# Of every two indirect transfers of GpSimd, only the first waits for a TensorE step

## The chip, the cores and the metric

The kernel runs on one core of one Trainium2 chip. The metric is the device time of one execution in microseconds (us), a median of several runs. A profiled execution has a span, from its first to its last instruction, and a time of its own that is a little longer. The engines are named as the profile names them: PE (TensorE; PEld its weight loads), DVE (VectorE), ACT (ScalarE), POOL (GpSimd) and SP (SyncE, which only issues DMAs here).

## What is computed

The first half is a gated recurrence over time, the second a mixture of eight experts in which each row goes to one expert.

```python
# x, f_logit: (4, 5056, 256); lower_bound: (256)
f = lower_bound + (1 - lower_bound) * sigmoid(f_logit)
for t in range(S):                       # S = 5056
    h = f[:, t] * h + (1 - f[:, t]) * x[:, t]
    y[:, t] = h
# y as N = 20224 rows of D = 256; E = 8 experts, F = 1024
xn, en = y / (norm(y) + 1e-6), emb / (norm(emb) + 1e-6)
logits = xn @ en.T / tau
e = argmax(logits); gate = softmax(logits)[e]
out[row] = gate * (relu(y[row] @ w1[e]) @ w2[e])
```

## The kernel before

**Chunks.** The 20224 rows are taken in 40 chunks of up to 512. For a chunk, SP loads f_logit and x (three buffers of each), TensorE transposes both so that features lie on partitions (L782, L816), ScalarE makes the gate (tanh, L793, and a scaled identity, L799), VectorE forms the product (L824) and scans along time (L840). ScalarE squares the result (L852). The result is turned back into rows, early on by TensorE, later by copies in bf16 (L861) and a DMA transpose on SP (L871), into the buffers `Yt`.

**Groups.** One or two chunks are a group. `route_` finds each row's expert and the slot that the row gets in its expert's region of a scratch in DRAM, `Xs`; `gate_` makes the gate weight, and then issues the scatters: for each block of 128 rows one indirect DMA on GpSimd's queue (L1109), which sends rows with gate and row number (544 bytes) to their slots. A full group has eight scatters, j = 0 to 7; there are 158 in all. `update_` writes, at chosen groups, a table of which expert's region the next tiles lie in.

**Tiles.** A tile is 256 rows of one expert. 81 tiles are always run (`NM`), a few more only if a counter asks for them. For tile n, SP loads the rows transposed from `Xs` (L1331; six buffers `ys`) and gate and row number (L1341, `xm`). TensorE multiplies by the expert's first matrix (L1434) in two steps, ScalarE and VectorE take the relu (L1455, L1460), TensorE multiplies by the second matrix (L1482) in four steps, ScalarE scales the first 128 rows by the gate (L1497) and VectorE the second 128 (L1501), into one of six buffers `osb`. Two indirect DMAs on GpSimd's queue (L1507), s = 0 and s = 1, send these to their rows of the output; there are 162.

**The order.** Nothing is ordered by hand. Each instruction group is an `Op` with dependencies, and `schedule` simulates all five engines with costs that are written beside the operations (an indirect transfer 1280 ns, a transfer's landing `DMA_FIX` 1900 ns) and places the operations one after another by readiness and priority. Each engine then runs its list in the order so found, and `resolve` turns each dependency into a semaphore wait, leaving out those that are implied by earlier waits. When an operation of GpSimd that carries a DMA and has `paced` set is placed at the simulated time s, it gets one more dependency, after its place is fixed: on the last TensorE step whose simulated end is not later than s (`PACE` is 0). On the chip GpSimd therefore does not run ahead of TensorE further than in the simulation. Before the change all scatters are paced, and all outputs except those of the last four tiles. GpSimd's other work is a set of constants at the start and the load of the sixteen expert matrices (L762).

Of the kernel before, what the change touches and what calls it, by code (L numbers as in the profile page):

```python
# [34 lines left out]
class Prog:  # L35
# [93 lines left out]
    def schedule(self, first, caps):  # L129
# [43 lines left out]
        while True:  # L173
            best = None
            for e in free:
                while wait[e] and wait[e][0][0] <= free[e]:
                    t, p, i, o = heapq.heappop(wait[e])
                    heapq.heappush(avail[e], (p, i, o))
                if avail[e]:
                    s = free[e]  # L180
                elif wait[e]:
                    s = wait[e][0][0]
# [6 lines left out]
            s, e = best  # L189
# [6 lines left out]
            if soon is not None:  # L196
                wait[e].remove(soon)
                heapq.heapify(wait[e])
                s, p, i, o = soon
            elif avail[e]:  # L200
                p, i, o = heapq.heappop(avail[e])
            else:
                t, p, i, o = heapq.heappop(wait[e])
            gap = s - free[e]
            if e == "pe" and s < self.COLD and gap > self.IDLE:
                room = [(t, q) for q, t in enumerate(frees) if t is not None and t <= s - self.IDLE]
                if room and ready_at(self.warm_on) is not None:
                    t, q = min(room)
                    a = max(t, free[e], ready_at(self.warm_on))
                    n = int((s - a - self.REST) / (self.UNIT * (2 if s < self.COLD else 1)))  # L210
# [29 lines left out]
            if o.dma is not None:  # L240
                bus = max(bus, free[e]) + o.nbytes / self.DMA_RATE
                o.end = max(bus, free[e]) + self.DMA_FIX
                if e == "pool" and o.paced:
                    o.end = min(o.end, free[e] + self.DMA_FIX)
            else:
                o.end = free[e] + self.LAG[e]
# [126 lines left out]
def bass_hgrn_recurrence__then__cosine_router_kernel(  # L373
# [41 lines left out]
    with ExitStack() as es:  # L415
# [491 lines left out]
        def views(g, hr=None):  # L907
            cc = groups[g]
            K, nb = len(cc), nof(cc[0]) // P
            J = K * nb  # L910
            q = g % R2
            o = bof[g][1] * 8

            def rt_():
                return bank[hr.b][:, 0:392].rearrange("p (b c) -> p b c", b=4)[:, 0:nb, :]

            def Lv():
                return rt_()[:, :, 0:64].rearrange("p b (k e) -> p b k e", k=2)[:, :, 0:K, 0:8]

            def Nv():  # L920
                return rt_()[:, :, 64:98:32][:, :, 0:K]

            def v4(t, o=0):
                return t[:, o * 8 : (o + J) * 8].rearrange("p (b k e) -> p b k e", b=nb, k=K)

            def v3(t, o=0):
                return t[:, o : o + J].rearrange("p (b k) -> p b k", b=nb)

            def bc(t, o=0):
                return v3(t, o).unsqueeze(3).to_broadcast([P, nb, K, 8])  # L930

            return K, nb, J, q, Lv, Nv, v4, v3, bc
# [115 lines left out]
        def gate_(bi):  # L1048
# [32 lines left out]
            for g in gg:  # L1081
                K, nb, J = views(g)[0:3]
                v3 = views(g)[7]
                o = bof[g][1] * 8
# [16 lines left out]
            for g in gg:  # L1101
                K, nb, J = views(g)[0:3]
                o = bof[g][1] * 8
                for b in range(nb):
                    for k_ in range(K):
                        j = b * K + k_
                        sc = op(
                            "pool",
                            lambda e, j=o + j, i=o + k_ * 4 + b: e.indirect_dma_start(  # L1109
                                out=Xs[:, :],  # L1110
                                out_offset=bass.IndirectOffsetOnAxis(
                                    ap=sli[y][:, j : j + 1], axis=0
                                ),
                                in_=Yt[y][:].bitcast(I32)[:, i, :],
                                in_offset=None,
                            ),
                            1280, r=[("Yt", y, k_, 0), ("Yt", y, k_, 1), ("Ytg", y), ("Yti", y), ("ytz", y), ("sli", y)],
                            w=[("Xs", g)], dma=f"sc{y}_{k_}", nbytes=100000, chain=False,
                        )
                        sc.paced = True  # L1120


        def update_(u, g, last):
# [188 lines left out]
        NM = N // T + E // 4  # L1312
# [5 lines left out]
        def tile_(j, u, g, n):  # L1318
# [105 lines left out]
            for mp in range(2):  # L1424
# [26 lines left out]
                for m, h in ((2 * mp, hh[0]), (2 * mp + 1, hh[1])):  # L1451
                    o = hT[qh][:, 2 * m : 2 * m + 2, :].rearrange("p f c -> p (f c)")
                    if m % 2 == 0:
                        act(
                            lambda e, o=o, h=h: e.activation(o, bank[h.b][:], AF.Relu), 512,  # L1455
                            h=h, w=[("hT", qh, m)], prio=EVP(pr.prio), tag="mid",
                        )
                    else:
                        dve(
                            lambda e, o=o, h=h: e.tensor_scalar(  # L1460
                                o, bank[h.b][:], 0.0, None, op0=ALU.max
                            ),
# [41 lines left out]
            for s in range(2):  # L1504
                sc = op(
                    "pool",
                    lambda e, s=s: e.indirect_dma_start(  # L1507
                        out=out[:, :],
                        out_offset=bass.IndirectOffsetOnAxis(
                            ap=xm[qx][:, s, 1:2], axis=0  # L1510
                        ),
                        in_=osb[qo][:, s, :],
                        in_offset=None,
                        bounds_check=N - 1,
                        oob_is_err=False,
                    ),
                    1280, r=[("osb", qo, s)] + xk, w=[("out", j, s)], dma=f"od{qo}_{s}",
                    nbytes=170000, prio=OUTP(pr.prio),
                )
                sc.paced = n < NM - 4  # L1520


        last_of = {cc[-1]: g for g, cc in enumerate(groups)}
# [20 lines left out]
        def put(j, n):  # L1544
            u, g = avail[j]
            pr.prio = 10000 + n
            tile_(j, u, g, n)

        for c in range(NCH):
            pr.prio = c  # L1550
            if c >= 2:
                load(c)
            F_(c)
            X_(c)
            Y_(c)
            if c == 0:
                for i in range(2 * E):
                    wload(i, c)
            if c == 1:
                late_constants()  # L1560
            if c in last_of:
                g = last_of[c]
                route_(g)
                bi, gi = bof[g]
                if g == batches[bi][-1]:
                    gate_(bi)
                for u, at in enumerate(ups):
                    if at == g:
                        update_(u, g, u == len(ups) - 1)
# [63 lines left out]
```

## Time and profile before

| | us |
|---|---|
| three timed runs | 559.63, 563.5, 564.1 |
| their median | 563.5 |
| the profiled execution's own time | 565.46 |
| its span | 563.7 |
| PE busy / PEld busy | 475.2 / 382.8 |
| DVE busy | 359.5 |
| ACT busy | 321.1 |
| POOL busy | 331.9 |

Busy time is summed over the span; engines work beside each other, so the rows don't add up to it. The granted TensorE clock was 0.963 of full speed on average. The last chunk's scan lies near 332 us, so that the last 230 us hold tiles alone, with the rest of the scatters between their outputs.

### The profile page before, as it was taken

To read this page: it belongs to the slowest core of one execution; us is meant where nothing else is said; L and a number is where in the kernel's file an instruction comes from. 1 tells how busy PE (TensorE), PEld (TensorE's weight loads), DVE (VectorE), ACT (ScalarE), POOL (GpSimd) and SP (SyncE) were. 2 spreads that over 40 slices of the span, in tenths; PEclk is the share of its full clock that TensorE was granted. 3 is DMA by queue.
4 is the path that set the end of the run, shared out by engine and by line. 5 is a ranking of instruction groups with operands and counts; after the bars stand their busy time and mean duration, and the time that the engine had idled before them with its cause. 6 is when DMAs were issued, how large, how long until landed. Compare 5 with 4: busy or idle time off the path is not lost. (4 is left out here: it accounts for less than half of the span.)

```text
span 563.7 us, 12407 instructions
## 1 busy us (share of the span) xinstructions
PE 475.2 (84%) x4106; PEld 382.8 (68%) x4106; DVE 359.5 (64%) x1075; ACT 321.1 (57%) x573; POOL 331.9 (59%) x388
## 2 busy tenths in 40 slices
PE   7796778979798789887887988888988897978994
PEld 4474557757577567656765657777777776867894
DVE  7869978877787667875877876533444343443452
ACT  4878768877787566757776753333333332333342
POOL 6164565655665565564666665656665666655555
PEclk8969988998998889999999999999999999999998
DMA  8999999999999788879896543353343433444422
GB/s 243 302 311 313 318 254 311 287 254 219 206 234 241 202 205 190 238 172 219 221 241 133 117 92 99 113 127 105 100 110 95 110 88 100 106 109 101 106 65 74
DMA packets 119681, 100.49 MB, mean 178 GB/s; under 512 B 96884, under 2 KB 98687, under 8 KB 119616
## 3 DMA queue, kind: packets, MB, share of 16 engines
q1 hardware_dynamic: 101664, 59.38, 42.5%
q0 software_dynamic: 16224, 40.26, 26.2%
q8 instruction: 36, 0.59, 0.5%
q10 hardware_dynamic: 1728, 0.01, 0.2%
q14 instruction: 29, 0.24, 0.2%
HBM read 59.21 MB, written 32.93 MB: 163 GB/s over the span
## 5 line engine op out<-in xcount | busy, mean ns | idle before, releaser
L1507 POOL DMA_INDIRECT out_dram<-osb,xm x162 | 160.7, 992 | 107.6 <-issue 34.0
L1109 POOL DMA_INDIRECT XsScratch<-Yt,sli x158 | 152.2, 963 | 105.6 <-issue 26.6
L1434 PE MATMUL bank<-ys,wall 128*128 128x256 bf16 (+1 forms) x1392 | 174.4, 271 | 19.1 <-issue 13.4
L1482 PE MATMUL bank<-wall,hT 128*128 x1296 | 172.8, 274 | 15.0 <-issue 12.6
L1460 DVE TENSOR_SCALAR hT<-bank 128x512 bf16<-128x512 f32 x162 | 108.4, 684 | 100.8 <-remote 46.0
L1434 PEld LDWEIGHTS bank<-ys,wall 128*128 x1392 | 147.5, 145 | 34.9 <-issue 24.7
L1455 ACT ACTIVATE hT<-bank 128x512 bf16<-128x512 f32 x162 | 94.0, 597 | 114.1 <-remote 49.5
L1482 PEld LDWEIGHTS bank<-wall,hT 128*128 128x128 bf16 x1296 | 124.4, 98 | 42.9 <-issue 23.0
L840 DVE TENSOR_TENSOR_SCAN hb<-fg,hb,bank 128x512 f32<-128x512 f32 (+4 forms) x78 | 95.9, 1236 | 0.1
L1501 DVE TENSOR_SCALAR osb<-bank,xm 128x256 f32<-128x256 f32 x81 | 38.8, 479 | 59.7 <-ACT osb L1497 32.6
L1497 ACT ACTIVATE osb<-bank,xm 128x256 f32<-128x256 f32 x81 | 38.4, 475 | 59.7 <-remote 17.4
L816 PE MATMUL bank<-ident,xin 128*128 128x128 f32 x316 | 53.2, 294 | 22.7 <-ACT fg L799 12.9
L799 ACT ACTIVATE fg<-th,cs 128x512 f32<-128x512 f32 (+1 forms) x80 | 64.4, 812 | 1.4 <-DVE cs L627 0.2
L816 PEld LDWEIGHTS bank<-ident,xin 128*128 128x128 f32 x316 | 37.7, 149 | 34.6 <-ACT fg L799 16.9
L824 DVE SCALAR_TENSOR_TENSOR bank<-fg,bank 128x512 f32<-128x512 f32 (+1 forms) x80 | 54.1, 680 | 9.6 <-PE bank L816 6.8
L793 ACT ACTIVATE th<-bank 128x512 f32<-128x512 f32 (+1 forms) x80 | 46.3, 592 | 22.7 <-PE bank L782 14.2
L782 PE MATMUL bank<-ident,fin 128*128 128x128 f32 x316 | 53.5, 300 | 4.5 <-DMA fin<-in_f_logit_dram 2.0
L782 PEld LDWEIGHTS bank<-ident,fin 128*128 128x128 f32 x316 | 40.4, 155 | 12.2 <-issue 4.5
L852 ACT ACTIVATE sq<-hb 128x1024 f32<-128x1024 f32 (+1 forms) x40 | 41.8, 1045 | 2.0 <-DVE hb L840 1.6
L945 PE MATMUL bank<-hb,eT 128*8 128x512 f32 (+1 forms) x160 | 41.7, 599 | 0.3 <-issue 0.3
L949 PE MATMUL bank<-sq,onesf 128*1 128x512 f32 (+1 forms) x160 | 41.5, 597 | 0.0
L861 ACT ACTIVATE hbf<-hb 128x512 bf16<-128x512 f32 x50 | 31.4, 629 | 4.7 <-DVE hb L840 4.2
(139 smaller groups left out, 305.3 us busy)
## 6 DMA issues: line engine op xcount, KB each, us to landing
fin<-in_f_logit_dram SPq DMA_DIRECT2D x39, 512.0 KB
xin<-in_x_dram SPq DMA_DIRECT2D x39, 512.0 KB
wall<-in_moe_w_dram POOLq DMA_DIRECT2D x16, 512.0 KB, 10.6
out_dram<-osb,xm POOLq DMA_INDIRECT x162
XsScratch<-Yt,sli POOLq DMA_INDIRECT x158
ys<-XsScratch SPq DMA_TRANSPOSE x81
xm<-XsScratch SPq DMA_DIRECT2D x75, 2.0 KB
osb<-XsScratch SPq DMA_DIRECT2D x6, 136.0 KB
```

The source lines that it names most:

```text
L782: i = e.transpose(bank[h.b][:, b : nb * P : nb], fin[q][:, b, dh * P : (dh + 1) * P], ident[:],)
L793: lambda e, dh=dh, h=h: e.activation(th[dh][:, 0:n], bank[h.b][:, 0:n], AF.Tanh, scale=0.5),
L799: lambda e, dh=dh: e.activation(fg[c % 2][:, dh, 0:n], th[dh][:, 0:n], AF.Identity, bias=cs[:, dh, 0:1], scale=cs[:, dh, 1:2],),
L816: i = e.transpose(bank[h.b][:, b : nb * P : nb], xin[q][:, b, dh * P : (dh + 1) * P], ident[:],)
L824: lambda e, dh=dh, h=h: e.scalar_tensor_tensor(out=bank[h.b][:, 0:n], in0=fg[c % 2][:, dh, 0:n], scalar=1.0, in1=bank[h.b][:, 0:n], op0=AL ...
L840: lambda e, dh=dh, s0=s0, s1=s1, init=init, h=h: e.tensor_tensor_scan(hb[c % NH][:, dh, s0:s1], fg[c % 2][:, dh, s0:s1], bank[h.b][:, s0:s ...
L1109: lambda e, j=o + j, i=o + k_ * 4 + b: e.indirect_dma_start(out=Xs[:, :], out_offset=bass.IndirectOffsetOnAxis(ap=sli[y][:, j : j + 1], axis=0
L1434: i = e.matmul(bank[hh[f // 2].b][:, at : at + R_], wall[:, bass.ds(a1[j, s][(4 * mp + f) * DT + kt] - WA - WREV, 2 * FT * P),].bitcast(BF ...
L1455: lambda e, o=o, h=h: e.activation(o, bank[h.b][:], AF.Relu), 512,
L1460: lambda e, o=o, h=h: e.tensor_scalar(o, bank[h.b][:], 0.0, None, op0=ALU.max),
L1482: i = e.matmul(po(s), hT[qh][:, kf, s * P : (s + 1) * P], wall[:, bass.ds(a2[j, s if last else 0][kf] - WA, 2 * D)].bitcast(BF16), start=( ...
L1507: lambda e, s=s: e.indirect_dma_start(out=out[:, :], out_offset=bass.IndirectOffsetOnAxis(ap=xm[qx][:, s, 1:2], axis=0), in_=osb[qo][:, s, :],
```

## The change

The flag `paced` now is set for every second transfer only: for the scatters of a group those with even j, for the outputs those with s = 0 (again without the last four tiles). A transfer without it waits for its data only. So that the simulation does not change with it, the line that shortens a paced transfer's simulated end now asks for the name of the DMA (`sc...` a scatter, `od...` an output) in place of the flag.

```diff
@@ schedule
             if o.dma is not None:
                 bus = max(bus, free[e]) + o.nbytes / self.DMA_RATE
                 o.end = max(bus, free[e]) + self.DMA_FIX
-                if e == "pool" and o.paced:
+                if e == "pool" and o.dma[:2] in ("sc", "od"):
                     o.end = min(o.end, free[e] + self.DMA_FIX)
@@ gate_
                             w=[("Xs", g)], dma=f"sc{y}_{k_}", nbytes=100000, chain=False,
                         )
-                        sc.paced = True
+                        sc.paced = j % 2 == 0
@@ tile_
-                sc.paced = n < NM - 4
+                sc.paced = s == 0 and n < NM - 4
```

## Rows read from the trace of the kernel before

**Rows 1.** Busy time by stage: PE, PEld, DVE, ACT, POOL (instructions), PEclk, DMA share, GB/s.
```profile
17.00:100.00 83.00, 64.42 (x524) 48.46 (x524) 69.01 (x247) 64.68 (x106) 43.99 (x49) 0.88 1.04 303
100.00:200.00 100.00, 86.41 (x764) 69.04 (x757) 76.03 (x239) 75.44 (x133) 59.05 (x61) 0.95 0.96 233
200.00:300.00 100.00, 84.88 (x739) 64.70 (x738) 74.74 (x225) 69.14 (x121) 59.84 (x62) 0.98 0.85 207
...
350.00:450.00 100.00, 87.50 (x741) 75.63 (x740) 41.79 (x85) 34.72 (x70) 61.92 (x64) 1.00 0.42 109
450.00:550.00 100.00, 89.75 (x842) 79.32 (x841) 42.78 (x74) 37.29 (x74) 58.77 (x61) 1.00 0.40 97
```
**Rows 2.** PE's waits, 17 to 100 us, then 350 to 550: us, times, longest.
```profile
PE bank L816 <- ACT fg L799: 9.1, 7, 2.8
PE bank L1013 <- DVE oh L996: 3.7, 3, 1.6
...
PE bank L1482 <- issue: 10.8, 21, 1.2
PE bank L1434 <- issue: 9.6, 23, 1.1
```
**Rows 3.** The page: busy times, the two indirect groups (busy, mean ns, idle before), queues.
```profile
PE 475.2 (84%) x4106; PEld 382.8 (68%) x4106; DVE 359.5 (64%) x1075; ACT 321.1 (57%) x573; POOL 331.9 (59%) x388
...
L1507 POOL DMA_INDIRECT out_dram<-osb,xm x162 | 160.7, 992 | 107.6 <-issue 34.0
L1109 POOL DMA_INDIRECT XsScratch<-Yt,sli x158 | 152.2, 963 | 105.6 <-issue 26.6
...
q0 software_dynamic: 16224, 40.26, 26.2%
q8 instruction: 36, 0.59, 0.5%
```
**Rows 4.** The waits of SP's queue over the span: us, times, longest.
```profile
SPq L1329 <- PE bank L1434: 52.1, 26, 5.2
SPq L585 <- PE bank L816: 34.4, 14, 4.2
SPq L1329 <- remote: 25.8, 9, 4.3
...
SPq L585 <- PE bank L782: 19.8, 9, 5.9
```
**Rows 5.** The chain that ended last: start, us, what.
```profile
559.96 0.30 issue
560.26 0.98 POOL out_dram L1507
```
**Rows 6.** Timelines of POOL, SP, DVE, 460 to 515 us: start, us, [idle before <-releaser].
```profile
480.07 0.98 POOL L1507 DMA_INDIRECT out_dram<-osb,xm  x1 [1.71 <-PE bank L1434]
...
482.62 0.96 POOL L1109 DMA_INDIRECT XsScratch<-Yt,sli  x1 [0.30 <-issue]
...
513.02 0.98 POOL L1507 DMA_INDIRECT out_dram<-osb,xm  x1 [2.30 <-DVE hT L1460]
514.31 0.99 POOL L1507 DMA_INDIRECT out_dram<-osb,xm  x1 [0.30 <-issue]
...
491.73 5.79 SPq L1331 DMA_TRANSPOSE ys<-XsScratch  x3
...
463.59 0.48 DVE L1501 TENSOR_SCALAR osb<-bank,xm 128x256 f32<-128x256 f32 x1 [0.21 <-ACT osb L1497]
...
489.96 0.48 DVE L1501 TENSOR_SCALAR osb<-bank,xm 128x256 f32<-128x256 f32 x1
```
**Rows 7.** Timeline of the end, from 552 us.
```profile
553.07 3.66 PE L1482 MATMUL bank<-wall,hT 128*128 x32
...
553.80 0.98 POOL L1507 DMA_INDIRECT out_dram<-osb,xm  x1 [2.27 <-DVE osb L1501]
555.09 0.99 POOL L1507 DMA_INDIRECT out_dram<-osb,xm  x1 [0.30 <-issue]
```
**Rows 8.** Lines L1507 and L1109: duration ns min/median/max, first and last start.
```profile
L1507 POOL DMA_INDIRECT out_dram<-osb,xm x162: 983/992/1008, 108.0 to 560.3; - x162
...
L1109 POOL DMA_INDIRECT XsScratch<-Yt,sli x158: 952/959/1059, 27.5 to 482.6; - x158
```

## The prediction

> **What bounds the kernel now.** I read the stages first [rows 1]. After the first 17 us the kernel has two regimes. Up to 300 us the chunks are loaded, scanned, routed and scattered while tiles are already computed: TensorE is busy 64.4 of 83 us, then 86.4 and 84.9 of 100 us, VectorE 69.0 of 83 and then about 75 of 100, and the DMA engines run at a share of 1.04, 0.96 and 0.85. From 350 to 550 us only tiles and the last scatters are left: TensorE 177.3 of 200 us (the two stages of 87.50 and 89.75 together), VectorE and ScalarE under half, DMA at 0.4, granted clock 1.00. GpSimd is busy 59 to 62 of every 100 us from 100 us on and nowhere full.
>
> Then what ends TensorE's idle time [rows 2]. From 17 to 100 us it is mostly ScalarE's gate (9.1 us) and VectorE's one-hot (3.7 us); nothing there is released by GpSimd. From 350 to 550 us, 20.4 of 22.7 us idle (10.8 + 9.6, in 44 places) are ended by nothing that the profile shows ("issue"). No line says that TensorE waits for a tile's rows.
>
> Then who depends on GpSimd. Its two indirect lines hold 312.9 of its 331.9 us [rows 3]. SP, which loads the tiles' rows from the scratch that GpSimd scatters into, sits longest for TensorE steps (52.1, 34.4 and 19.8 us: a buffer that is still being read), and 25.8 us are put down to a releaser that the profile doesn't name [rows 4]. The chain of waits is two pieces long, GpSimd's last output and 0.30 us before it, because it stops where the profile names no releaser [rows 5]; so it says that the last thing is an output, not what set the other 560 us. That I take from the stages: TensorE with the vector chain up to about 300 us, TensorE with its own issue stalls after it.
>
> **The change, part by part.**
>
> (1) *The waits that go.* The first of a pair keeps its wait on a TensorE step; the second loses it: 79 of 158 scatters (odd j) and 77 of 162 outputs (s = 1 of tiles 0 to 76; the last four tiles waited for no such step before either). What does such a wait cost? Back to back, an indirect transfer takes 0.96 to 0.99 us and the next begins 0.30 us later, so 0.30 us is no stall [rows 6]. The idle time before the two lines is 107.6 + 105.6 us [rows 3]; 320 x 0.30 = 96 us of that is the fixed gap, which leaves about 117 us of true waiting. Going down the timeline of GpSimd and counting the transfers of each line alternately, I find 46 us of it before seconds (26.3 us at 21 outputs, 19.7 us at 26 scatters) and 69 us before firsts, 115 in all; the seconds of [rows 6] at 480.07 us (1.71 us idle before it) and 513.02 us (2.30) are of the first kind. Their data can be old by then: the one at 480.07 us is the second output of tile 57 (46 outputs come after it), and its scaling on VectorE, the 24th counted from the end, began at 463.59 us, 16 us earlier [rows 6]. So nearly all of the 46 us can go from *that* place.
>
> (2) *Where the stall goes.* The next first still waits for its own TensorE step, and the planner puts its start at least one transfer (1.28 us in its costs) later. With the wait before a second gone, that second starts up to 2.3 us earlier, and the next first is late next. It starts when its step is done or the second has ended, whichever comes last. On 513.02 us: the second could go 2.0 us earlier (2.30 less the fixed 0.30), at 511.02, and the first behind it at its step or at 512.3, so the transfers behind it move by at most 2.0 us until the next wait takes it back. I put the net at 1 us earlier, over trains of three to five transfers. GpSimd's rate doesn't change: it has 60 of 100 us of work in either kernel, and TensorE steps still hold every second transfer.
>
> (3) *Who gains from transfers that are 1 us earlier.* Three consumers. First, the tile loads from scratch: the last scatter ends at 482.62 + 0.96 = 483.58 us and the first load that needs all scatters comes with the three loads from 491.73 us [rows 6]: 8.1 us lie between them, and by [rows 4] it is TensorE freeing a buffer that SP waits for. Second, the output buffers (six, used in turn): tile 57's second output is sent at 480.07 us, and tile 63 writes the same buffer at 489.96 us [rows 6], 8.9 us after the transfer's end; GpSimd is at its latest there (by the same count of outputs against scalings), so elsewhere the room is larger. Third, the end: the last eight outputs don't change at all. GpSimd stands idle for 2.27 us ahead of 553.80 us, so it has caught up, and sends six more, 1.29 us apart, to 561.24 us [rows 7]; only what moves TensorE's last step, at 553.07 + 3.66 us, moves these. So the gain on the path is 0 us by all three; the cover is 8 to 9 us deep, and what would have to be gone for the change to matter is that room, not 1 us of it.
>
> (4) *What it adds.* No instruction; about one semaphore instruction less ahead of an output. GpSimd's queue order stays: the TensorE step is attached after an operation has been placed, and the planner's end for scatters and outputs keeps the same formula, except for the last eight outputs, whose end now feeds only the closing no-ops. On SP, ScalarE and VectorE nothing is moved. The transfers come closer together in time, mostly with no more than two between TensorE steps; the bytes stay (40.26 MB of the software queue, which also carries the weights) [rows 3].
>
> A rule of the Trainium skill speaks against letting GpSimd run freer. The rows first: over all of a line's instances the outputs took 983/992/1008 ns and the scatters 952/959/1059 ns (least, median, most) [rows 8], beside a VectorE that is 64% busy [rows 3]. In the skill's "SBUF — State Buffer", section "SBUF: two separate sides", GpSimd cannot write the descriptors of its own transfers while VectorE holds the port pair that the two share. By that rule a second that no longer starts with a step could be stretched by a VectorE instruction; the trace differs, as no transfer is stretched by more than 0.1 us wherever it fell. By the rule the 1 us of (2) would be lost again and the sum would be the old 563.5 us; by the rows it stands.
>
> The sum: 565.46 us is the profiled execution's own time (563.7 us span and 1.8 us around it); 0 us on the path by (3), at most 1 us if a train's gain leaks through. The three timed runs are 559.63, 563.5 and 564.1 us, so the profiled one lies 2 us over their median; from the median and half a microsecond of leak I forecast **563.0 us**.
>
> **The rivals.**
>
> *A: GpSimd's lateness is on the path after all.* For it: at 480 us GpSimd is 16 us behind VectorE, and 25.8 us of SP's waits have no named releaser [rows 4]. If tile loads or buffers wait for late transfers, the stalls before seconds in the tile regime count in full: 13.3 + 4.2 + 7.9 = 25 us from 350 to 560 us, and by (2) perhaps a third of it isn't given back to the next first: 8 us, 555 us. Against it: TensorE's list has no such wait in that regime [rows 2], and by 553.80 us the lag is gone [rows 7] with no engine's wait put down to it.
>
> *B, slower: released transfers get into TensorE's instruction supply.* The place is 350 to 550 us, the 44 issue stalls of 20.4 us [rows 2]; the instruction queue's 36 packets use the same 16 DMA engines as all else [rows 3]. If seconds now run beside a refill which the wait used to keep them from, each stall lengthens. It decides (over 1%) from 5.6 us, when stalls grow by 27%; at 40% it is +8 us, 571 us. For it: a step that is late makes the second wait now, so a second that is set free runs just while TensorE stands. Against it: the DMA share is only 0.4 there [rows 1], and six transfers go out 1.29 us apart at the end without harm to be seen [rows 7]. The skill's "Runtime: NRT & Kernel Launch", section "Instruction fetch mechanics", has each engine refill in 16 KiB blocks and calls the crossing mostly hidden; by that B would give nothing. The trace differs: 20.4 us of TensorE's idle time there have no other cause in view.
>
> *C: it does not do what it says.* If the TensorE step is implied by what a second waits for anyway (its VectorE scaling, data of the scatter), the 46 us stay where they are: 563.5 us. Against it: the data of the one at 480.07 us was 16 us old. Its time is that of the forecast.
>
> *D: the clock.* From 17 to 100 us the granted clock is 0.88 and from 100 to 200 us 0.95 [rows 1], a mix of the levels 1.2 and 2.4 GHz. At 0.88 over 83 us at most 10 us of TensorE's pace are missing there. Scatters that come earlier shift who waits when, and a third of that either way is 3 us, within what the three runs already span (4.5 us). It widens the range and has no sign.
>
> **How the numbers follow.** Forecast, C and D as one outcome, 559 to 567 us: 0.70. A: 0.15, 551 to 558 us. B: 0.13, 569 to 580 us. Two in a hundred are left for what I have not named. A measurement of this kernel tells about 1% (5.6 us) from no change. The range reaches from the forecast's 559 us into the near half of A and from 567 us into the near part of B: 555.5 to 570 us. Faster by over 1%: 0.16 (A and a little); slower by over 1%: 0.14; within 1%: 0.70.
>
> **What the changed profile would show.** Step 1: the idle time before the two GpSimd lines falls from 213 us, yet by less than 46 us; among seconds few idles of over 0.4 us are left. Step 2: idle of one to two microseconds stands before firsts, more often than now. Step 3: the last scatter starts one or two microseconds ahead of 482.6 us, the lag at 480 us shrinks, and TensorE's busy time from 350 to 550 us stays at 177 us within 2, with 20 us of issue stalls. Step 4: transfers of 0.96 and 0.99 us as now. Wrong would be: tile loads moving with the scatters (A), issue stalls of 27 us or more at the same DMA bytes (B), or a granted clock from 17 to 200 us off by 0.03 or more (D).

## The result, and the profile after

The changed kernel takes 570.91 us (median of six runs, 567.64 to 574.2) beside 561.76 us (559.63 to 564.1) of the kernel before: a ratio of 1.0147, with an interval of 1.0102 to 1.0192. It is slower by about 9 us; I had forecast 563.0 us and no difference that can be measured. Medians here are of all runs of a kernel; ratios leave out its executions that took over 1.5% more than its fastest.

One thing has to be known before any number of this case is read. The kernel before itself runs at one of two levels: in some sets of runs its median is 471 to 474 us, in others 562 to 570 us, and none of its executions lies between 480 and 557 us. Every ratio of the experiments is between runs of one set, and so of one level. For the pair above the record names no set; both its sides, and both traces, are of the upper level. Since the kernel before alone moves by 8 us from set to set there, the 1.0147 is safe only if both sides come from one set.

The stages after, to be held against [rows 1] (PE, PEld, DVE, ACT and POOL busy with their instructions, granted clock, DMA share, GB/s):

```profile
17.00:100.00 83.00, 64.37 (x538) 46.78 (x534) 69.92 (x247) 65.75 (x107) 45.62 (x51) 0.92 1.04 306
100.00:200.00 100.00, 85.21 (x772) 69.01 (x773) 79.16 (x248) 76.48 (x136) 60.56 (x62) 0.98 0.99 240
200.00:300.00 100.00, 81.51 (x720) 63.69 (x719) 71.74 (x216) 67.73 (x118) 58.01 (x60) 0.98 0.84 199
350.00:450.00 100.00, 87.96 (x713) 74.37 (x712) 40.78 (x81) 33.48 (x67) 59.25 (x61) 0.95 0.43 105
450.00:550.00 100.00, 88.50 (x806) 78.53 (x804) 40.41 (x69) 35.86 (x69) 57.76 (x59) 0.97 0.41 96
```

The surprise is in the last two rows: TensorE's busy time is nearly that of before (176.5 for 177.3 us), but it holds 1519 matmuls for 1583, and the granted clock is 0.95 and 0.97 where it was 1.00. Where the time goes can be dated from two ScalarE lines, here of before and then of after (duration least/median/most, first and last start):

```profile
L852 ACT ACTIVATE sq<-hb x40: 622/1055/1074, 14.5 to 332.6; 128x1024 f32<-128x1024 f32 x39, 128x512 f32<-128x512 f32 x1
...
L1497 ACT ACTIVATE osb<-bank,xm x81: 457/474/494, 106.4 to 555.9; 128x256 f32<-128x256 f32 x81
```

```profile
L852 ACT ACTIVATE sq<-hb x40: 622/1054/1103, 14.9 to 330.6; 128x1024 f32<-128x1024 f32 x39, 128x512 f32<-128x512 f32 x1
...
L1497 ACT ACTIVATE osb<-bank,xm x81: 454/474/490, 104.9 to 561.0; 128x256 f32<-128x256 f32 x81
```

L852 works on the chunks: its last start comes 2.0 us *earlier* than before. L1497 works on the tiles: its last start comes 5.1 us later. So the whole loss, 7 us, arises after 331 us, where only tiles and the last scatters are left. The same from the rows of the stretch 340 to 552 us, before and then after:

```profile
340.00:552.00 212.00, 187.90 (x1686) 164.26 (x1684) 93.09 (x216) 75.34 (x151) 128.64 (x131) 1.00 0.40 102
```

```profile
340.00:552.00 212.00, 187.57 (x1618) 162.08 (x1617) 89.58 (x195) 74.61 (x148) 124.00 (x127) 0.96 0.41 100
```

68 matmuls fewer, at 0.111 us of busy time each (187.90 / 1686), are 7.6 us, while TensorE stands no longer than before: what was lost is pace, not idle time. The waits of TensorE from 350 to 550 us say the same. They sum to 21.4 us in 40 places, beside 20.4 us in 44 in [rows 2]:

```profile
PE bank L1434 <- issue: 11.0, 24, 1.1
PE bank L1482 <- issue: 10.4, 16, 1.1
```

One place shows what lies behind it. The timeline of after from 411 us, TensorE, GpSimd and one instruction of ScalarE:

```profile
411.03 1.00 POOL L1507 DMA_INDIRECT out_dram<-osb,xm  x1 [0.30 <-issue]
411.96 0.43 PE L1434 MATMUL bank<-ys,wall 128*128 128x256 bf16 x2 [0.45 <-issue]
...
412.79 0.98 POOL L1507 DMA_INDIRECT out_dram<-osb,xm  x1 [0.76 <-DVE hT L1460]
413.39 0.43 PE L1434 MATMUL bank<-ys,wall 128*128 128x256 bf16 x2 [0.32 <-issue]
414.08 0.99 POOL L1507 DMA_INDIRECT out_dram<-osb,xm  x1 [0.30 <-issue]
414.81 0.86 PE L1434 MATMUL bank<-ys,wall 128*128 128x256 bf16 x4 [0.99 <-issue]
415.37 0.96 POOL L1109 DMA_INDIRECT XsScratch<-Yt,sli  x1 [0.30 <-issue]
...
418.20 0.47 ACT L1497 ACTIVATE osb<-bank,xm 128x256 f32<-128x256 f32 x1
...
418.50 1.90 PE L1434 MATMUL bank<-ys,wall 128*128 128x256 bf16 x8 [0.21 <-ACT hT L1455]
419.46 0.99 POOL L1507 DMA_INDIRECT out_dram<-osb,xm  x1 [3.13 <-DVE osb L1501]
```

And the longest stall but one of the kernel before, at 420 us, with one instruction of VectorE ahead of it:

```profile
417.27 0.47 DVE L1501 TENSOR_SCALAR osb<-bank,xm 128x256 f32<-128x256 f32 x1
...
420.49 0.96 POOL L1109 DMA_INDIRECT XsScratch<-Yt,sli  x1 [0.30 <-issue]
...
421.76 0.99 POOL L1507 DMA_INDIRECT out_dram<-osb,xm  x1 [0.30 <-issue]
422.00 0.27 PE L1434 MATMUL bank<-ys,wall 128*128 128x256 bf16 x1 [0.27 <-issue]
...
424.22 1.03 PE L1482 MATMUL bank<-wall,hT 128*128 x8
425.02 0.99 POOL L1507 DMA_INDIRECT out_dram<-osb,xm  x1 [2.27 <-ACT osb L1497]
```

In both, TensorE's matmuls come in twos and ones with "issue" between them. Before, GpSimd meets a wait after 421.76, sends nothing for 2.27 us, and TensorE is back at full pace at 424.2. After, it keeps sending, four transfers from 411.03 to 415.37 us; TensorE is back at 418.50, some 2 us after the last of them has ended, and eight matmuls take 1.90 us in place of 1.03. What held the transfers has to be counted out, as the names in the brackets mislead here. The one at 425.02 is the second output of tile 46, whose scaling began at 417.27 and was 7 us old: it waited for its TensorE step, and the ACT named is the scaling of the next output. The one at 419.46 is the first output of tile 45, whose scaling began only at 418.20, when TensorE was back: it waited for its data. The windows around this stall give the clock (columns as above):

```profile
405.00:411.00 6.00, 6.00 (x58) 5.64 (x57) 2.17 (x5) 1.61 (x4) 4.50 (x5) 1.00 0.48 111
411.00:415.00 4.00, 2.00 (x12) 1.07 (x11) 0.69 (x1) 0.60 (x1) 2.91 (x3) 1.00 0.27 98
415.00:421.00 6.00, 5.26 (x24) 3.00 (x23) 2.87 (x5) 2.50 (x5) 2.26 (x4) 0.50 0.23 60
422.00:428.00 6.00, 6.00 (x57) 5.52 (x55) 1.32 (x3) 1.82 (x4) 2.95 (x3) 1.00 0.61 122
```

First the stall at full clock, with TensorE busy half the time; then the lower level (0.50, that is 1.2 of 2.4 GHz), with TensorE busy nearly throughout again at half pace. Before, the whole stretch from 340 to 552 us stands at 1.00. Counting weight loads more than 0.5 us apart in the timeline, and taking such gaps as one stall where only a dozen loads or fewer lie between them, I find 26 stalls before that lose 33.6 us, the longest 4.4 us long, and 20 stalls after that lose 33.9 us, the longest 7.5 us (the one above). **The stalls cost the same in sum; they are fewer, some are longer, and behind four of them the clock is low**, for 17 us together. At half pace that is at most 8.5 us. By the 69 matmuls that begin in it, each 0.11 us longer than at full clock, it is 7.5 us, which covers the 7. Over the whole span the low clock hardly grew: from 17 to 331 us it fell from 34 to 20 us, and the mean of the profiled executions is 0.961 for 0.963.

The two indirect lines of the page, beside those of [rows 3]:

```profile
L1507 POOL DMA_INDIRECT out_dram<-osb,xm x162 | 160.9, 993 | 119.5 <-issue 34.5
L1109 POOL DMA_INDIRECT XsScratch<-Yt,sli x158 | 152.5, 965 | 98.1 <-issue 31.2
```

### The profile page after: what moved, and what is told of

Read it like the earlier page. It is cut to its first block, busy times and chain, and to the rows that moved or that the text cites. A ratio compares the mean times of both kernels' runs of the same rounds, so it can differ in the third digit from the quotient of the medians.

```text
span 568.8 us, 12353 instructions
## 1 busy us (share of the span) xinstructions
PE 475.7 (84%) x4106; PEld 383.5 (67%) x4106; DVE 359.9 (63%) x1075; ACT 322.1 (57%) x573; POOL 332.5 (58%) x388
## 5 line engine op out<-in xcount | busy, mean ns | idle before, releaser
L1507 POOL DMA_INDIRECT out_dram<-osb,xm x162 | 160.9, 993 | 119.5 <-issue 34.5
L1109 POOL DMA_INDIRECT XsScratch<-Yt,sli x158 | 152.5, 965 | 98.1 <-issue 31.2
L1434 PE MATMUL bank<-ys,wall 128*128 128x256 bf16 (+1 forms) x1392 | 176.4, 272 | 24.5 <-issue 12.3
L1482 PE MATMUL bank<-wall,hT 128*128 x1296 | 174.6, 278 | 13.0 <-issue 11.1
L1460 DVE TENSOR_SCALAR hT<-bank 128x512 bf16<-128x512 f32 x162 | 108.4, 684 | 84.8 <-remote 33.5
L1482 PEld LDWEIGHTS bank<-wall,hT 128*128 128x128 bf16 x1296 | 125.9, 99 | 41.6 <-issue 21.4
L1455 ACT ACTIVATE hT<-bank 128x512 bf16<-128x512 f32 x162 | 93.9, 597 | 102.7 <-PE bank L1434 43.8
L1497 ACT ACTIVATE osb<-bank,xm 128x256 f32<-128x256 f32 x81 | 38.4, 474 | 83.8 <-issue 28.3
L816 PE MATMUL bank<-ident,xin 128*128 128x128 f32 x316 | 51.8, 288 | 25.7 <-ACT fg L799 15.7
L782 PE MATMUL bank<-ident,fin 128*128 128x128 f32 x316 | 51.3, 292 | 6.6 <-issue 4.0
L852 ACT ACTIVATE sq<-hb 128x1024 f32<-128x1024 f32 (+1 forms) x40 | 41.8, 1046 | 2.0 <-DVE hb L840 1.6
```

Of the source, the lines that this page charges most:

```text
L782: i = e.transpose(bank[h.b][:, b : nb * P : nb], fin[q][:, b, dh * P : (dh + 1) * P], ident[:],)
L816: i = e.transpose(bank[h.b][:, b : nb * P : nb], xin[q][:, b, dh * P : (dh + 1) * P], ident[:],)
L1109: lambda e, j=o + j, i=o + k_ * 4 + b: e.indirect_dma_start(out=Xs[:, :], out_offset=bass.IndirectOffsetOnAxis(ap=sli[y][:, j : j + 1], axis=0
L1434: i = e.matmul(bank[hh[f // 2].b][:, at : at + R_], wall[:, bass.ds(a1[j, s][(4 * mp + f) * DT + kt] - WA - WREV, 2 * FT * P),].bitcast(BF ...
L1460: lambda e, o=o, h=h: e.tensor_scalar(o, bank[h.b][:], 0.0, None, op0=ALU.max),
L1482: i = e.matmul(po(s), hT[qh][:, kf, s * P : (s + 1) * P], wall[:, bass.ds(a2[j, s if last else 0][kf] - WA, 2 * D)].bitcast(BF16), start=( ...
```

## The experiments

Four theories stand in the expectations. *Theory 1*, the wait as a brake: a GpSimd transfer that waits for a TensorE step can't start while TensorE stalls, so the waits keep transfers out of the stalls, and the stalls short. *Theory 2*: the clock fell by chance, the waits do nothing. *Theory 3*: GpSimd's lateness itself counts. *Theory 4*: any stall will do, and has nothing to do with TensorE's instructions: a transfer without a wait gets ahead in it and costs time by its traffic or by late buffers. The instructions stand in the same order on every engine in all kernels that differ in the waits alone; of 340 indirect transfers (20 of them conditional) 283 wait for a TensorE step before, 273 in "tight", 228 in "halfout", 155 after, 0 in "none".

**All waits away, the scatters' or the outputs' alone, and tighter ones.**

```diff
# each of these has the planner's line of the change
# none
-sc.paced = True
+sc.paced = False
-sc.paced = n < NM - 4
+sc.paced = False
# halfout: only the outputs of the change
-sc.paced = n < NM - 4
+sc.paced = s == 0 and n < NM - 4
# halfsc: only the scatters of the change
-sc.paced = True
+sc.paced = j % 2 == 0
# tight: waits for the last TensorE step planned to end up to 1 us after the transfer's start
-PACE = 0.0
+PACE = -1000.0
```

> No scatter and no output waits for a TensorE step any more; nothing else differs. Theory 1 (feedback): when TensorE's instructions are late, the wait on its step stops GpSimd, and TensorE comes back about 1 us after GpSimd's last transfer has ended; a transfer that doesn't wait prolongs the stall by 1.3 us. Then stalls get longer still than with half of the waits: time 578 us or more (before 562, half of the waits 571), longest stall of TensorE in the tile regime over 8 us, granted clock from 350 to 550 us below 0.95. Theory 2 (the clock alone: the 7 us lost in the tile regime come from low-clock stretches that fall there by chance, whatever waits): time 562 to 574 us, stalls as with half of the waits. Theory 3 (GpSimd's lateness is what counts, and the change only shuffled it): without waits the transfers are earliest, so 555 to 562 us.

> Only the outputs half of the change: all scatters wait as before, of a tile's outputs only the first waits. Theory 1: outputs are 22 to 30 of some 30 transfers of each 50 us in the tile regime, where the loss sits, so most of it is here: 567 to 571 us. Theory 2: 561 to 571 us, no order between this run and the scatter half. If the loss came from scatters that are sent early among the loads, this run would stand at 562 us.

> Only the scatters half of the change: all outputs wait as before, of a pair of scatters only the first waits. Theory 1: from 340 us on only some 29 scatters are left, so little of the loss: 561 to 566 us, below the outputs half. Theory 2: 561 to 571 us. If early scatters among the loads were the cause: 571 us.

> All scatters and outputs wait as in the kernel before, but for a later TensorE step: the last one whose planned end is no later than 1 us after the transfer's planned start (the kernel before: no later than the start). Queue orders are the same. Theory 1: GpSimd stops sooner when TensorE stalls, stalls get shorter: 553 to 560 us, longest stall in the tile regime below 4 us, clock 1.00 there. Theory 2: no change beyond 1%, 558 to 568 us. Theory 3 (lateness of GpSimd counts): later transfers, 565 us or more.

Measured: 470.44, 470.98, 471.96 and 471.68 us, the kernel before 471.9 us in the same set. Ratios 0.9982 [0.9945, 1.0019], 0.9969 [0.9935, 1.0004], 0.9989 [0.9955, 1.0022], 0.998 [0.9942, 1.0018]: nothing differs, not even without any wait. The set was at the lower level, and the traces say why it could tell nothing. "None" and then the changed kernel (next experiment) at that level:

```profile
300.00:450.00 150.00, 150.00 (x1443) 142.29 (x1441) 75.37 (x129) 70.81 (x129) 109.95 (x112) 1.00 0.55 127
```

```profile
300.00:450.00 150.00, 150.00 (x1442) 142.26 (x1441) 75.38 (x129) 70.97 (x129) 111.74 (x114) 1.00 0.56 127
```

TensorE is busy 150.00 of 150 us: there is no issue stall to be shortened or drawn out, and none of the 13 runs at this level has one from 300 to 450 us. What follows is a condition, that the waits cost or gain nothing where TensorE doesn't stall.

**The changed kernel once more, and stalls put in by hand.** The second edit sets 64 no-ops on TensorE's queue ahead of every third tile, in the kernel before (e6) and in the changed one (e7).

```diff
+if s == 0 and n % 3 == 2:
+    for _ in range(64):
+        e.nop()
```

> The changed kernel itself once more, for a second trace. The four runs of the first experiment took 470 to 472 us, the kernel before too, and TensorE had no issue stall from 300 to 450 us in them. Theory 1 (the change costs time only where TensorE's instructions come late): if the kernel before takes about 472 us here and TensorE has no issue stalls, the ratio is within 0.995 to 1.005; if it takes about 562 us with issue stalls, the ratio is 1.01 to 1.02, with stalls of 5 us and more and low-clock stretches in the tile regime. Theory 2 (the clock by chance): a ratio of 0.99 to 1.02 in either case, not tied to stalls.

> The kernel before (all scatters and outputs wait for a TensorE step) with 64 no-operations on TensorE's queue ahead of every third tile, 27 places: TensorE then stands still for some 2 to 4 us there, as it does at its issue stalls in the trace of before, but for a reason that GpSimd's transfers can't touch. On a chip where the kernel before takes 472 us: 472 plus 27 times the stall, 520 to 570 us. The number that counts is how the next run stands to this one.

> The changed kernel (of every two transfers the first waits) with the same 64 no-operations ahead of every third tile. Theory 1 (the changed kernel lost because transfers that don't wait make an issue stall longer): these stalls have a length of their own, so the time is that of the run with all waits within 0.5%. Theory 4 (any stall of TensorE will do: when it stands, a second transfer that doesn't wait gets ahead and costs time by its traffic or by late buffers, without any part of TensorE's instruction supply): 1 to 2% slower than the run with all waits. Theory 2 (the clock falls after stalls by chance): both within 1%, with low-clock stretches in both.

Measured: the changed kernel 471.3 beside 471.64 us, 1.0002 [0.9963, 1.0041], again at the lower level. With the no-ops, at the upper level, 569.53 and 575.79 us beside 568.34: 1.0056 [1.0006, 1.0106] and 1.0122 [1.0039, 1.0205]. In the kernel before the no-ops cost 1 to 3 us in all (1.2 us by the medians, 0.6% by the ratio), so they are no stalls worth the name and the question they were put to stays unanswered. But the two kernels are a second pair of "all" and "half" waits. In time it settles nothing: 1.0122 / 1.0056 is 1.007, the intervals overlap, and the two profiled executions lie 0.8 us apart (569.36 and 570.16 us). In the clock it has the pattern of the first pair. Their tile regime, e6 and then e7:

```profile
340.00:552.00 212.00, 185.13 (x1641) 161.61 (x1639) 91.65 (x204) 73.31 (x148) 125.87 (x128) 0.99 0.40 100
```

```profile
340.00:552.00 212.00, 187.70 (x1616) 162.83 (x1616) 90.27 (x194) 73.66 (x147) 124.19 (x127) 0.96 0.41 100
```

The low clock is there for 3.4 us in e6 and for 17 us in e7, as in the first pair; yet from the last start of L852 to the end of the tiles e7 takes only 2.0 us more.

**"None" and "tight" until a set fell on the upper level.**

> No scatter and no output waits for a TensorE step, once more: the first time this kernel met a chip on which TensorE's instructions are never late (472 us, all kernels alike); it tells the theories apart only on a chip where the kernel before takes 560 to 570 us. There, theory 1 (waits bound how long an issue stall lasts): 1.02 to 1.05 of before, longest stall in the tile regime over 6 us, granted clock there below 0.96. Theory 2 (chance): 0.99 to 1.02. Theory 3 (early transfers help): below 1.00. On the other kind of chip: within 0.995 to 1.005 by all.

> Every scatter and output waits for a TensorE step planned to end up to 1 us later than in the kernel before. On a chip where before takes 560 to 570 us, theory 1: 0.97 to 1.00 of before, longest stall in the tile regime below 4.5 us, clock 0.98 or more there; the run without waits is slower than this by 3% or more. Theory 2: both runs within 1% of each other. Theory 3: slower than before, and slower than the run without waits. On the other kind of chip: within 0.995 to 1.005 by all.

> No wait at all, a third time, in search of a chip on which the kernel before takes 560 to 570 us. There, theory 1 (waits bound how long an issue stall lasts): 1.02 to 1.05 of before, longest stall in the tile regime over 6 us, granted clock there below 0.96. Theory 2 (chance): 0.99 to 1.02. Theory 3 (early transfers help): below 1.00. On the other kind of chip: within 0.995 to 1.005 by all.

> Each wait for a TensorE step planned up to 1 us later than before, a third time. On a chip where before takes 560 to 570 us, theory 1: 0.97 to 1.00 of before, longest stall in the tile regime below 4.5 us, clock 0.98 or more there. Theory 2: within 1% of the run without waits. Theory 3: slower than the run without waits. On the other kind of chip: within 0.995 to 1.005 by all.

> No wait at all, once more in search of a chip on which the kernel before takes 560 to 570 us; one kernel alone, compared by its ratio to before with the changed kernel's 1.0147. There, theory 1 (waits bound how long an issue stall lasts): 1.02 to 1.05, longest stall in the tile regime over 6 us, granted clock there below 0.96. Theory 2 (chance): 0.99 to 1.02. Theory 3 (early transfers help): below 1.00. On the other kind of chip: within 0.995 to 1.005 by all.

> Each wait for a TensorE step planned up to 1 us later than in the kernel before. The run without any wait has shown 1.12 of before on a chip where before takes 562 us, with long stalls and a clock of 0.91 in the tile regime, as theory 1 has it (the waits stop GpSimd's transfers while TensorE is stalled, and so bound the stall). On such a chip theory 1 gives here 0.97 to 1.00, longest stall in the tile regime below 4.5 us, clock 0.98 or more there; if GpSimd's lateness cost time as well (theory 3), over 1.01. On a chip where before takes 472 us: 1.00 to 1.01.

At the lower level once more: e8 0.9998 [0.9975, 1.0021], e9 1.0014 [0.9969, 1.0058], e10 1.0005 [0.9973, 1.0037], e11 1.0067 [1.0025, 1.0109] (outside the 0.995 to 1.005 that all theories had for this level), e13 1.0006 [0.9972, 1.0041]. At the upper level, **e12: 632.08 us without any wait, beside 561.79 us, 1.1215 [1.1146, 1.1284]**. This is the largest number of the study: the waits that seemed to cost GpSimd 115 us of idle time are worth 70 us to the kernel. Its stages, the chunks' squares, and TensorE's waits from 350 to 550 us:

```profile
17.00:100.00 83.00, 57.93 (x468) 43.13 (x465) 63.79 (x227) 57.27 (x93) 45.29 (x51) 0.86 1.02 292
100.00:200.00 100.00, 76.16 (x611) 59.67 (x610) 62.24 (x191) 64.15 (x110) 43.10 (x45) 0.85 0.71 180
...
450.00:550.00 100.00, 83.47 (x637) 69.03 (x637) 35.04 (x60) 31.05 (x60) 58.50 (x61) 0.91 0.37 93
```

```profile
L852 ACT ACTIVATE sq<-hb x40: 620/1052/1075, 14.3 to 387.0; 128x1024 f32<-128x1024 f32 x39, 128x512 f32<-128x512 f32 x1
```

```profile
PE bank L1434 <- issue: 13.8, 27, 1.1
PE bank L1482 <- issue: 10.1, 21, 1.1
```

From 450 to 550 us there are 637 matmuls where before there are 842, at 83.47 us of busy time for 89.75; the clock is 0.91. The two lines of issue waits hardly grow (23.9 us in 48 places), but they are not all of it: from 350 to 550 us TensorE is idle for 36 us where before it is 23, and by the count of weight loads the stalls lose 50 us for 32, the first 37 of the 200 us still having chunks in them. Unlike the change, "none" loses most while the chunks are loaded: the last start of L852 falls at 387.0 us for 332.6, 54 of the 70 us. No experiment takes that part apart, so that it comes by the same way as the loss among the tiles is not shown. At GpSimd itself nothing was gained by freeing it: 43.10 us busy from 100 to 200 us, for 59.05. What it meets in place of the TensorE steps is its data: of 58 outputs with over 0.5 us of idle time before them, 52 start 0.78 to 0.83 us after their own scaling has ended.

Theory 2 falls with this for the kernel without waits, as the waits do something there; that the 1.5% of the change is more than the clock's chance does not follow from it. Theory 3 falls, by which the kernel without waits should have been the fastest. Theory 1 has the order right, with 1, 1.0147 and 1.1215 for 283, 155 and 0 waits at the upper level, but not the size: it gave 1.02 to 1.05 here.

**The parts, at the upper level.**

> Only the outputs half of the change (all scatters wait, of a tile's outputs only the first), again in search of a chip on which the kernel before takes 560 to 570 us. There, theory 1: outputs are three quarters of the transfers in the tile regime, where the changed kernel lost its 7 us, so most of the 1.47% is here: 1.007 to 1.015. If the scatters carried it: 0.997 to 1.005. Theory 2 (chance) is out by the run without waits. On the other kind of chip: 0.995 to 1.005.

> Only the scatters half of the change: all outputs wait, of a pair of scatters only the first. The outputs half has just shown 1.0005 (0.9962 to 1.0049) on a chip where before takes 570 us, against what theory 1 expected of it. On such a chip: if the two halves add up, the scatters carry the 1.47% and this run stands at 1.010 to 1.018. If it takes both (a run of transfers without a wait only becomes long when an output and a scatter that don't wait stand next to each other), this run is at 0.997 to 1.006. On the other kind of chip: 0.995 to 1.005.

> Only the scatters half of the change, again in search of a chip on which before takes 560 to 570 us. Over the whole list GpSimd has 283 transfers with a TensorE wait in the kernel before, 228 with the outputs half (1.0005), 215 here, 155 with both (1.0147), 0 without any (1.12). If the halves add up, this run carries it: 1.010 to 1.018. If only both together make runs of three transfers without a wait common: 0.997 to 1.006. On the other kind of chip: 0.995 to 1.005.

> Each wait for a TensorE step planned up to 1 us later than in the kernel before (273 transfers with a TensorE wait in place of 283), again in search of a chip on which before takes 560 to 570 us. There, if the wait sets how long a stall lasts, stopping GpSimd earlier gives 0.97 to 0.99, with a longest stall in the tile regime below 4.5 us and a clock of 0.98 or more; if the stalls' floor is already reached with the waits of before, 0.99 to 1.01; if GpSimd's lateness costs time, above 1.01. On the other kind of chip: 0.995 to 1.007.

> Only the scatters half of the change, a last time in search of a chip on which before takes 560 to 570 us. If the halves add up, this run carries the loss: 1.010 to 1.018. If only both together make runs of three transfers without a wait common: 0.997 to 1.006. On the other kind of chip: 0.995 to 1.005.

e14 fell on the upper level: 571.04 beside 569.82 us, 1.0005 [0.9962, 1.0049]. The outputs' half of the change does nothing that can be measured, against my expectation. In its trace no idle is left before second outputs, and the stretch 340 to 552 us (the first row below, e17 in the second) has 6.8 us of low clock and 1624 matmuls, nearly as few as after. As the kernel before stood at 569.82 us in that set, and has no trace of it, only the ratio can be used. e17 too: 564.89 beside 562.01 us, 1.0033 [0.9996, 1.0071]; tighter waits gain nothing, though the longest stall in the tile regime is 3.6 us and the clock 0.98, as theory 1 had it for a gain of 1 to 3%.

```profile
340.00:552.00 212.00, 186.42 (x1624) 161.66 (x1625) 92.22 (x222) 73.72 (x147) 126.79 (x129) 0.98 0.41 102
```

```profile
340.00:552.00 212.00, 186.47 (x1668) 164.87 (x1667) 90.96 (x196) 75.39 (x149) 126.67 (x130) 0.98 0.42 101
```

The three tries of the scatters alone (0.9963 [0.9916, 1.001], 0.9984 [0.9937, 1.003], 1.0003 [0.9962, 1.0044]) all fell on the lower level. Whether the scatters' half carries the loss alone, or only both halves together, stays open. No version beats the kernel before.

**All traces of the upper level side by side.** Stalls are counted as above, from 340 to 552 us (e12: 400 to 612 us, behind its last chunk). "Begun" is how many indirect transfers start within a stall; "tiles" is the time from the last start of L852 to that of the tiles' scaling on ScalarE (L1497; L1500 in e6 and e7).

| trace | waits | longest stall, us | lost in stalls, us | begun | low clock, us | tiles, us |
|---|---|---|---|---|---|---|
| e17 tight | 273 | 3.6 | 34 | 16 | 6.8 | 225 |
| before | 283 | 4.4 | 34 | 10 | 0 | 223 |
| e6, no-ops | 283 | 4.2 | 36 | 17 | 3.4 | 228 |
| e14 halfout | 228 | 6.5 | 35 | 15 | 6.8 | 227 |
| after | 155 | 7.5 | 34 | 15 | 17.1 | 230 |
| e7, no-ops | 155 | 5.8 | 35 | 14 | 17.1 | 230 |
| e12 none | 0 | 6.8 | 40 | 22 | 23.9 | 239 |

With all the waits the longest stall is 3.6 to 4.4 us and the clock is low for 0 to 6.8 us; with fewer it is 5.8 to 7.5 us, with 6.8 to 23.9 us of low clock, in one trace of each. But the link that theory 1 is named for does not show between all and half of the waits: as many transfers begin within stalls with all of them (10, 16 and 17) as with half (14 and 15). Only without any wait are there more.

## Why the prediction was wrong

**The step that failed is (3): "So the gain on the path is 0 us by all three".** The three were consumers of GpSimd's transfers, and none of them shows up: of TensorE's waits from 350 to 550 us, all but 1.5 us (two places each at L1460 and L1455, the ReLU of its own sums) are issue stalls. What I left out of the sum there is the engine that consumes nothing of them: TensorE's own pace among the tiles, where its clock stood at 1.00, is no term of that sum, and so was put at nothing. Measured, the clock there is 0.96, 17 us of it low behind four of the longer stalls, and the missing term is +7 us in the tile regime in the profiled pair, +9 us in the medians. That the change brings these longer stalls is what the two pairs of traces agree on; by which way it does stays open.

**Step (1) was right in place.** The idle time before seconds, 46 us, is gone: none is left at either line. Its count of waits was too high: it takes the flag from 156 transfers, but only 128 waits go (283 to 155), as the others were implied by earlier ones. **Step (2) was right in direction and too small.** The idle before firsts grew from 69 to 120 us, since every stall that a second used to sit through now meets the next first, and longer. So "the idle time before the two GpSimd lines falls from 213 us" was wrong: it is 217.6 us (119.5 + 98.1). "The last scatter starts one or two microseconds ahead" was wrong as well: it starts at 485.03 us, 2.4 us later, with TensorE's steps. The statement "GpSimd's rate doesn't change" held. **Step (4) held**: the transfers last 993 and 965 ns for 992 and 963. So the rule of the Trainium skill in "SBUF — State Buffer", section "SBUF: two separate sides", shows no price here either.

**Rival B came nearest, with its price in the wrong term.** Its place (350 to 550 us) and its sign are what the runs bear out. Its reason ("a step that is late makes the second wait now, so a second that is set free runs just while TensorE stands") they do not: 15 transfers begin within stalls after, and 10, 16 and 17 with all the waits. And I had it decide when the issue stalls' sum grows by 27%, and that sum grew by 1.0 us, 5%. What I had named as its sign would have let me reject it. What changed is the length of single stalls: four of the longer ones are followed by a stretch at the lower clock, and the cost lies in busy time, 0.116 us a matmul (176.5 / 1519) for 0.112 (177.3 / 1583). Against B I had held the last six transfers, 1.29 us apart without harm; they prove little, as TensorE has only its last 32 matmuls left beside them [rows 7]. I gave B 0.13 and an end of 570 us to the range; the median lies 0.9 us beyond it.

**Rival D** had the clock right and its stage wrong. I looked for it from 17 to 200 us, where after is at 0.92 and 0.98 for 0.88 and 0.95, *better* than before, and where the kernel is indeed 2 us ahead; so D's sign (0.03 or more) was met there, in the direction that gains. The loss came where the clock had been 1.00 throughout and seemed no term at all. **A** fell: e12 has GpSimd freest and is slowest. **C** fell: the idle time left the seconds.

"Mostly hidden" is what the Trainium skill calls the crossing from one block of instructions to the next ("Runtime: NRT & Kernel Launch", section "Instruction fetch mechanics"). Two levels were measured here: at the lower one no issue stall is seen in 150 us, at the upper one 20.4 us in 200. That the stalls are that crossing is not shown by any run, and the packets of the instruction queue speak against the simplest form of it: at the two longest stalls after (411.0 to 418.5 and 461.6 to 467.1 us) none of its 36 packets of 16 KiB begins within the stall, the next ones begin at 420.9 and 469.4 us, and one takes 0.9 to 1.9 us there and 0.9 to 1.7 us in e5, at the lower level, without stalls.

What remains argued and not shown: that a GpSimd transfer holds up TensorE's issue at all, and why it would. The traces show the order in time at single stalls (GpSimd sends on, the stall lasts; GpSimd stops, TensorE returns about 2 us later), which would be the same if GpSimd stopped because TensorE did, and the number of waits against time (283, 155 and 0; the 228 of the outputs' half cost nothing). The stalls put in by hand, which were to tell theory 1 from theory 4, failed as a means, so theory 4 is open. That stalls in sum make the clock fall does not fit, as stalls of the same sum (33.6 and 33.9 us) go with 0 and 17 us of low clock. Length alone isn't the whole of it either: a stall of 4.4 us before, at 493 us, leaves the clock at 1.00, and one of 2.9 us after, at 378 us, is followed by the lower level.

## What to carry to other kernels

A wait that looks like pure loss on its own engine can be worth time to the kernel. Before taking one out, ask not only who consumes what comes earlier, but what else goes on at the moment when the wait holds, and price a clock that stands at 1.00 as something that can be lost. Take all of such waits out as a test: half of them moved the time by 1.5%, all by 12%. And make sure that the runs contain the thing tested: 13 runs at the lower level showed six different kernels within 1% of each other.

## What the runs showed of the hardware

The same program has two levels, 471 and 562 to 570 us, and holds one through a set of runs. At the lower, TensorE is busy without a gap from 300 to 450 us; at the upper, it stands 11% of the tile regime, in stalls some 60 weight loads apart. One and the same chip showed both (number 9 in e14 and e15, number 11 in e13 and e17), so the level belongs to the set and not to the chip. What sets it is open. It is worth 19%, and within the upper level the kernel before itself moved from 561.8 to 569.8 us from set to set, so that a ratio across sets would have been worth nothing for a change of 1.5%.
